# Warm-up matmuls that read a preamble constant and last until x arrives, and a 384 + 256 split of the last output projection

## The chip, the cores and the metric

The kernel runs on one core of a Trainium2 chip. The metric is the device time of one execution in microseconds (us), the slowest core's, which here is the only one. Several executions of each kernel were timed; all of them count as fast runs (each lists a mean granted clock of 1.0).

## The reference

A gate mixes two branches of the same input x (2048 tokens of 640 features, bf16). Branch A is a diagonal complex state-space recurrence (P = 640 states) with an output projection; branch B is a two-layer network with a hidden width of 1728.

```python
g = sigmoid((x * gate_w).sum(-1, keepdims=True))
# A: Lam_bar = exp(dt * Lam); h_t = Lam_bar * h_{t-1} + B_bar x_t
#    y = 2 * Re(C h) + x * Dskip
# B: b = gelu(x @ w1 + b1) @ w2 + b2
return g * a + (1 - g) * b          # bf16, [1, 2048, 640]
```

## The kernel before

Every operation is recorded with its reads and writes. A small list scheduler orders the operations of each engine before anything is emitted, and semaphore waits follow from the reads and writes. Four parts matter here.

The first loads. `xtrans` is a transposing DMA of some 128-feature slices of x; `w1load(k, ...)` loads slice k of w1, its first 1024 columns, 256 KB. SP is SyncE, which issues DMAs.

```python
w1load(0, "act", -101)               # ScalarE's queue
xtrans(0, [0], 0, 1.27)              # all else on SP's queue, in this order
xtrans(0, [1, 2], 1, 1.27)
w1load(1, "sp", 2)
w1load(2, "sp", 3)
xtrans(0, [3, 4], 4, 1.27)
w1load(3, "sp", 5)
w1load(4, "sp", 6)
# ... five small loads into `rows` (Lambda, log_dt, b1) on ScalarE's queue
```

The warm-up: eight matmuls on zeros, which VectorE writes first. Their result is never read.

```python
wz = SB("wz", [128, 512], BF16)
def f_wz():
    return inc("dve", nc.vector.memset(wz[:, :], 0.0))
op("wz", "dve", 0.35, (), ["wz"], f_wz, prio=-70)

def f_warm():
    t = None
    for _ in range(8):
        t = nc.tensor.matmul(PS[6][:, :], wz[:, 0:128], wz[:, :], start=True, stop=True)
    return inc("pe", t)
op("warm", "pe", 3.2, ["wz"], [("bank", 6)], f_warm, prio=-1000)
```

The first real matmuls go slice by slice through x (k outer, eight output banks inner), so that TensorE can start with slice 0. Seven of them need only slice 0. After these comes `cols`, one small matmul that transposes `rows`; then those that need slice 1.

```python
seq = [(k, jf) for k in range(KD) for jf in range(NW)]
seq.remove((0, NW - 1))
seq.insert(seq.index((1, NW - 1)), (0, NW - 1))
# ... one matmul PS[jf] += W1sb[k, jf].T @ xT[0][k] for each
op("cols", "pe", 0.3, list(ROWS) + ["b1b", "ident"], [("bank", 7)], f_cols, prio=7.5)
```

The end. For the last chunk of 128 tokens, each half of the output projection (ten accumulating matmuls) is evicted by VectorE, which adds what was prepared before (`E2`), and is stored at once.

```python
# HALF = 320; NCH - 1 is the last chunk
for hf in range(2):
    cols = slice(hf * HALF, (hf + 1) * HALF)
    def f_fin(hf=hf, cols=cols):
        return inc("dve", nc.vector.scalar_tensor_tensor(
            out=osb[c % NO][:, cols], in0=PS[cbank[hf]][:, 0:HALF], scalar=gcol[:, c:c + 1],
            in1=E2[c % NE][:, cols], op0=ALU.mult, op1=ALU.add))
    def f_st(hf=hf, cols=cols):
        return dma_inc("sp", nc.sync.dma_start(o2[c * 128:(c + 1) * 128, cols], osb[c % NO][:, cols]), f"stl{hf}")
```

## Time and profile before

| | us |
|---|---|
| median of 3 executions | 214.95 (214.95 to 215.01) |
| span of the profiled execution | 213.84 |
| start of TensorE's dense run | 7.39 |
| start of the last VectorE operation | 211.61 |
| from there to the end of the span | 2.23 |

The page's busy times (busy us, share of the span, instructions), and, further down on it, its chain that ended last by engine. PE is TensorE's matmuls, PEld its weight loads, DVE VectorE, ACT ScalarE.

```profile
PE 210.0 (98%) x1257; PEld 119.3 (56%) x1257; DVE 188.3 (88%) x260; ACT 112.9 (53%) x205; POOL 2.5 (1%) x10
...
PE 95%; DMA 2%; SPq 1%; DVE 0%; issue 0%
```

TensorE bounds the kernel; only the first 7.4 us and the last 2.2 are anything else. The beginning of the chain in order of time (start in us, duration in us, what):

```profile
2.03 1.29 SPq L332
3.32 0.05 issue
3.37 3.89 DMA W1sb<-in_B_w_dram
7.26 0.14 issue
7.39 7.28 PE ps L598 x33
```

SP issues the transposing loads first, so the load of W1 slice 1 is issued at 3.37 and lands at 7.26; TensorE's unbroken work starts 0.13 us later. What TensorE did until then, from the timeline (start, duration, engine, line, operation, tiles, count, idle time before and what ended it):

```profile
1.19 0.13 PEld L400 LDWEIGHTS ps<-wz 128*128 128x128 bf16 x2 [1.19 <-DVE wz L393]
...
1.20 3.59 PE L400 MATMUL ps<-wz 128*128 128x512 bf16 x8 [1.20 <-DVE wz L393]
...
4.81 0.13 PEld L598 LDWEIGHTS ps<-xT,W1sb 128*128 128x128 bf16 x2 [0.93 <-DMA xT<-in_A_x_dram]
...
5.22 0.15 PEld L598 LDWEIGHTS ps<-xT,W1sb 128*128 128x128 bf16 x1 [0.27 <-issue]
5.65 0.81 PEld L598 LDWEIGHTS ps<-xT,W1sb 128*128 128x128 bf16 x4 [0.28 <-issue]
...
6.79 0.22 PE L410 MATMUL ps<-ident,rows 128*128 128x128 bf16 x1
...
7.39 6.85 PE L598 MATMUL ps<-xT,W1sb 128*128 128x512 bf16 x31 [0.39 <-DMA W1sb<-in_B_w_dram]
```

The weight loads show the clock. While they come one each 0.43 us and take 0.15 us, TensorE runs slow; four of them within 0.81 us, as from 5.65 on, are fast (all but the first of these take 0.10 us). The trace's own clock record has the full clock from 5.76. All eight matmuls that can go ahead are through by 7.0; then TensorE waits for W1 slice 1. And the end of the timeline:

```profile
208.69 2.88 PE L791 MATMUL ps<-CT,H 128*128 128x320 bf16 x20
...
210.25 0.55 DVE L824 SCALAR_TENSOR_TENSOR osb<-ps,gcol,E 128x320 bf16<-128x320 f32 x1 [0.31 <-PE ps L791]
210.83 1.69 SPq L830 DMA_DIRECT2D out_dram<-osb  x2
211.61 0.55 DVE L824 SCALAR_TENSOR_TENSOR osb<-ps,gcol,E 128x320 bf16<-128x320 f32 x1 [0.81 <-PE ps L791]
```

(A line with x2 or more is merged: the SP line spans both store issues.)

### The profile page before, as it was taken

What the parts mean: (1) busy time and instruction counts of PE and PEld (TensorE: products, weight loads), DVE (VectorE), ACT (ScalarE), POOL (GpSimd) and SP (SyncE); (2) the same over time, 40 slices, a digit from 0 to 9 for tenths busy, and PEclk for the clock granted to TensorE, in tenths of its full rate; (3) what the DMA queues carried; (4) which work ended last, traced back from release to release, by engine and by line L of the source; (5) the groups of instructions that cost most, each with busy time, mean ns of one, the idle gap of its engine ahead of it and who ended that gap; (6) DMA issues with size and microseconds to landing.
All of it is one profiled execution on the core that took longest, in us unless ns stands there. A gap on an engine that the chain in (4) does not pass through costs nothing.

```text
span 213.8 us, 3098 instructions
## 1 busy us (share of the span) xinstructions
PE 210.0 (98%) x1257; PEld 119.3 (56%) x1257; DVE 188.3 (88%) x260; ACT 112.9 (53%) x205; POOL 2.5 (1%) x10
## 2 busy tenths in 40 slices
PE   7999999999999999999999999999999999999995
PEld 2344444444567675444467767444446777677673
DVE  1599999999999899999999999499999999988612
ACT  2569556679525334557835332556786554535230
POOL 1000000000000100000000010000000000000000
PEclk9999999999999999999999999999999999999999
DMA  7999699999000140000000023000000010000011
GB/s 138 297 271 192 142 364 271 224 191 204 0 0 3 61 153 3 31 0 0 0 3 31 0 49 138 32 0 0 3 0 2 0 34 31 31 34 31 31 34 31
DMA packets 30874, 16.35 MB, mean 76 GB/s; under 512 B 23948, under 2 KB 29964, under 8 KB 30860
## 3 DMA queue, kind: packets, MB, share of 16 engines
q1 hardware_dynamic: 30368, 14.57, 28.7%
q0 software_dynamic: 288, 1.31, 2.0%
q10 hardware_dynamic: 204, 0.27, 0.5%
q8 instruction: 10, 0.16, 0.4%
q14 instruction: 4, 0.03, 0.0%
HBM read 7.63 MB, written 2.62 MB: 48 GB/s over the span
## 4 chain that ended last, share of the span: by engine, by line
PE 95%; DMA 2%; SPq 1%; DVE 0%; issue 0%
PE ps L745 26%; PE ps L618 22%; PE ps L791 21%; PE ps L658 20%; PE ps L598 3%; DMA W1sb<-in_B_w_dram 2%; PE ps L759 1%; SPq L332 1%; PE ps L636 1%; DVE osb L824 0%
## 5 line engine op out<-in xcount | busy, mean ns | idle before, releaser
L745 PE MATMUL ps<-W2sb,Gl 128*128 128x320 bf16 x416 | 59.1, 299 | 0.0
L745 PEld LDWEIGHTS ps<-W2sb,Gl 128*128 128x128 bf16 x416 | 40.6, 98 | 16.5 <-ACT Gl L625 0.4
L618 PE MATMUL ps<-xT,W1sb 128*128 128x512 bf16 x220 | 48.1, 379 | 0.0
L791 PE MATMUL ps<-CT,H 128*128 128x320 bf16 x320 | 46.1, 299 | 0.0
L698 DVE TENSOR_TENSOR_SCAN W<-atab,V 128x1280 bf16<-128x1280 f32 x16 | 44.3, 2811 | 0.3
L658 PE MATMUL ps<-xT,BT 128*128 128x512 bf16 x200 | 43.8, 379 | 0.0
L773 ACT ACTIVATE E<-ps,g1col 128x320 bf16<-128x320 f32 x32 | 16.1, 526 | 42.2 <-PE ps L759 18.3
L791 PEld LDWEIGHTS ps<-CT,H 128*128 128x128 bf16 x320 | 30.7, 98 | 13.5 <-issue 1.8
L618 PEld LDWEIGHTS ps<-xT,W1sb 128*128 128x128 bf16 x220 | 21.5, 98 | 25.9
L625 ACT ACTIVATE Gl<-ps,cols 128x512 bf16<-128x512 f32 x44 | 29.7, 691 | 11.5 <-PE ps L618 11.5
L658 PEld LDWEIGHTS ps<-xT,BT 128*128 128x128 bf16 x200 | 19.4, 98 | 23.5 <-ACT Gl L625 0.4
L667 ACT ACTIVATE U<-ps 128x512 bf16<-128x512 f32 x40 | 23.6, 595 | 15.7 <-PE ps L658 15.6
L802 ACT ACTIVATE E<-ps,gcol 128x320 bf16<-128x320 f32 x30 | 15.7, 528 | 16.7 <-PE ps L791 16.6
L732 ACT ACTIVATE ps<-b2b 128x320 f32<-128x320 bf16 x32 | 14.0, 440 | 0.9
L460 DVE TENSOR_TENSOR osb<-xg,E 128x640 bf16<-128x640 bf16 x15 | 7.3, 487 | 7.8 <-ACT E L802 6.8
L810 DVE SCALAR_TENSOR_TENSOR xg<-xn,gcol,dsk 128x640 bf16<-128x640 bf16 x16 | 13.8, 882 | 0.4
L575 DVE SCALAR_TENSOR_TENSOR scr<-xn,gwb 128x640 bf16<-128x640 bf16 x16 | 13.2, 823 | 0.4
L460 DVE TENSOR_TENSOR H<-H,V 128x1280 bf16<-128x1280 bf16 x16 | 12.5, 821 | 0.3
L460 DVE TENSOR_TENSOR V<-V,W 128x1280 bf16<-128x1280 bf16 x16 | 12.5, 821 | 0.3
L460 DVE TENSOR_TENSOR V<-mr,U 128x2560 bf16<-128x2560 bf16 x8 | 11.9, 1489 | 0.2
L460 DVE TENSOR_TENSOR H<-c,W 128x2560 bf16<-128x2560 bf16 x8 | 11.9, 1488 | 0.1
L460 DVE TENSOR_TENSOR V<-s,W 128x2560 bf16<-128x2560 bf16 x8 | 11.9, 1484 | 0.0
(77 smaller groups left out, 101.2 us busy)
## 6 DMA issues: line engine op xcount, KB each, us to landing
out_dram<-osb SPq DMA_DIRECT2D x15, 160.0 KB, 1.8
W2sb<-in_B_w_dram SPq DMA_DIRECT2D x1, 2080.0 KB, 12.2
xn<-in_A_x_dram SPq DMA_DIRECT2D x2, 640.0 KB, 6.4
xn<-in_A_x_dram POOLq DMA_DIRECT2D x2, 640.0 KB, 4.8
W1sb<-in_B_w_dram SPq DMA_DIRECT2D x4, 256.0 KB, 4.1
W1sb<-in_B_w_dram SPq DMA_DIRECT2D x1, 880.0 KB, 6.1
W1sb<-in_B_w_dram ACTq DMA_DIRECT2D x1, 256.0 KB, 2.8
gwb<-in_gate_w_dram SPq DMA_DIRECT2D x1, 160.0 KB, 5.2
```

What stands on the lines that cost most here:

```text
L460: return inc("dve", nc.vector.tensor_tensor(out=o, in0=a, in1=b, op=o_))
L618: t = nc.tensor.matmul(PS[bank][:, :], W1sb[:, k, jf * 128:(jf + 1) * 128], xT[q][:, k, :], start=(k == 0), stop=(k == KD - 1))
L625: return inc("act", nc.scalar.activation(Gl[q % 2][:, jf, :], PS[bank][:, :], ACT.Gelu_apprx_tanh, bias=b1col[:, jf:jf + 1]))
L658: t = nc.tensor.matmul(PS[bank][:, :], BT[:, ci, kd, k * 128:(k + 1) * 128], xT[q][:, kd, :], start=(kd == 0), stop=(kd == KD - 1))
L667: return inc("act", nc.scalar.activation(dst, src, ACT.Copy, scale=1.0 if ci == 0 else -1.0))
L698: t = inc("dve", nc.vector.tensor_tensor_scan(out=g[:, ci, :], data0=a, data1=v[:, ci, :], initial=0.0, op0=ALU.mult, op1=ALU.add))
L732: return inc("act", nc.scalar.activation(PS[bank][:, 0:HALF], b2b[:, cols], ACT.Copy))
L745: t = nc.tensor.matmul(PS[bank][:, 0:HALF], Gl[q % 2][:, jf, t4 * 128:(t4 + 1) * 128], W2sb[:, jf, cols], start=False, stop=False, skip_gr ...
L773: return inc("act", nc.scalar.activation(E1[c % NE][:, cols], PS[bank][:, 0:HALF], ACT.Copy, scale=g1col[:, c:c + 1]))
L791: t = nc.tensor.matmul(PS[bank][:, 0:HALF], H[b % NHB][:, ci, k, s * 128:(s + 1) * 128], CT[:, ci, k, cols], start=(i == 0), stop=(i == 2 ...
L802: return inc("act", nc.scalar.activation(E2[c % NE][:, cols], PS[bank][:, 0:HALF], ACT.Copy, scale=gcol[:, c:c + 1]))
L810: return inc("dve", nc.vector.scalar_tensor_tensor(out=xg[c % 2][:, :], in0=xn[q % 2][:, c % 4, :], scalar=gcol[:, c:c + 1], in1=dsk[:, :] ...
```

## The change

The intent has two parts. The warm-up is to start as soon as TensorE may, without VectorE's memset, by reading a constant 1.0 that the preamble writes anyway, and it is to last until x is there, so that the clock does not meet a gap. At the end, the last part that is evicted and stored is to be smaller (256 instead of 320 columns), since its eviction and its store are followed by nothing that could hide them.

```diff
-        wz = SB("wz", [128, 512], BF16)
-        def f_wz():
-            return inc("dve", nc.vector.memset(wz[:, :], 0.0))
-        op("wz", "dve", 0.35, (), ["wz"], f_wz, prio=-70)
+        one = nc.const_aps.tensor(1.0, [128, 1], BF16)
 
         def f_warm():
             t = None
-            for _ in range(8):
-                t = nc.tensor.matmul(PS[6][:, :], wz[:, 0:128], wz[:, :], start=True, stop=True)
+            for n in (512,) * 9 + (192,):
+                t = nc.tensor.matmul(PS[6][:, 0:n], one.broadcast_to([128, 128]), one.broadcast_to([128, n]), start=True, stop=True)
             return inc("pe", t)
-        op("warm", "pe", 3.2, ["wz"], [("bank", 6)], f_warm, prio=-1000)
+        op("warm", "pe", 3.9, (), [("bank", 6)], f_warm, prio=-1000)
# ... cproj: the last chunk alone
+        CCOLS = (slice(0, D - 256), slice(D - 256, D))
-                cols = slice(hf * HALF, (hf + 1) * HALF)
+                cols = CCOLS[hf] if c == NCH - 1 else slice(hf * HALF, (hf + 1) * HALF)
+                n = cols.stop - cols.start
# ... 0:HALF becomes 0:n in its matmuls; f_fin and f_st use CCOLS[hf];
# ... fin{hf} names both halves of E2 as read
```

More of the change, by code (lines that the diff above doesn't have):

```diff
@@ L783, in cproj, with f_mm @@
                 cbank[hf] = bank
-                cols = slice(hf * HALF, (hf + 1) * HALF)
-                def f_mm(bank=bank, cols=cols):
+                cols = CCOLS[hf] if c == NCH - 1 else slice(hf * HALF, (hf + 1) * HALF)
+                n = cols.stop - cols.start
+                def f_mm(bank=bank, cols=cols, n=n):
                     t = None
@@ L790, in f_mm @@
                         for k in range(KP):
-                            t = nc.tensor.matmul(PS[bank][:, 0:HALF], H[b % NHB][:, ci, k, s * 128:(s + 1) * 128], CT[:, ci, k, cols],
+                            t = nc.tensor.matmul(PS[bank][:, 0:n], H[b % NHB][:, ci, k, s * 128:(s + 1) * 128], CT[:, ci, k, cols],
                                                  start=(i == 0), stop=(i == 2 * KP - 1))
@@ L794, in f_mm @@
                     return inc("pe", t)
-                op(f"c_{c}_{hf}", "pe", 2 * KP * d_mm(HALF), [("H", b % NHB), ("CT", 0), ("CT", 1)], [("bank", bank)], f_mm, prio=pe_prio())
+                op(f"c_{c}_{hf}", "pe", 2 * KP * d_mm(n), [("H", b % NHB), ("CT", 0), ("CT", 1)], [("bank", bank)], f_mm, prio=pe_prio())
                 if c == NCH - 1:
@@ L820, in comb @@
                 for hf in range(2):
-                    cols = slice(hf * HALF, (hf + 1) * HALF)
+                    cols = CCOLS[hf]
                     def f_fin(hf=hf, cols=cols):
-                        return inc("dve", nc.vector.scalar_tensor_tensor(out=osb[c % NO][:, cols], in0=PS[cbank[hf]][:, 0:HALF], scalar=gcol[:, c:c + 1],
+                        return inc("dve", nc.vector.scalar_tensor_tensor(out=osb[c % NO][:, cols], in0=PS[cbank[hf]][:, 0:cols.stop - cols.start], scalar=gcol[:, c:c + 1],
                                                                         in1=E2[c % NE][:, cols], op0=ALU.mult, op1=ALU.add))
-                    op(f"fin{hf}", "dve", d_dve(HALF), [("bank", cbank[hf]), ("E2", c % NE, hf)], [("osb", c % NO, hf)], f_fin, prio=-60)
+                    op(f"fin{hf}", "dve", d_dve(HALF), [("bank", cbank[hf]), ("E2", c % NE, 0), ("E2", c % NE, 1)], [("osb", c % NO, hf)], f_fin, prio=-60)
                     def f_st(hf=hf, cols=cols):
```

## The prediction

> **What bounds the kernel now.** TensorE. The page gives PE 98% busy of a 213.8 us span; the chain that ended last is 95% PE, which runs from 7.39 us to about 211.6 without a wait. The change touches only the two ends.
>
> *Front.* In the chain of waits the first 7.4 us are not PE: two transposing loads are issued on SP (0.75 to 3.32 us), a W1sb load is issued at 3.37 and landed by 7.26, PE starts at 7.39. The timeline shows the warm-up inside that time: 8 matmuls from 1.20 us (released by the memset of wz on VectorE), one each 0.43 us; x is there at 4.81. The weight loads tell the clock: 0.15 us each until 5.65, then 0.10, and from there matmuls come 0.21 us apart. So two or three of the seven real matmuls that need only the first slices of x and W1 run slow. Still all seven are through by about 6.8, the small transposing matmul by 7.0, and PE then waits 0.39 us for the second W1 slice. The Trainium skill ("TensorE: Matmul & The Clock Gate", Part 1) says that the clock is released after about 3.4 us of sustained activity, in a free-running window; this trace has 4.4 us from the first warm-up matmul to the fast rate.
>
> *Tail.* The last 20 matmuls start at 208.7, 0.136 us each for 320 columns, and end at 211.6; VectorE's last operation takes 0.551 us (211.61 to 212.16); the store is issued at 212.19 and lands 1.6 us later, which ends the span.
>
> **What the change does.**
> 1. The wz memset (0.27 us) and the wait for it go. PE may start at about 0.85 to 0.95, some 0.3 us earlier. 9.4 matmuls at 0.427 are 4.0 us, so warm-up ends at about 4.9, just past 4.81. Real matmuls may begin up to 0.1 us later, or the fast clock may come 0 to 0.3 us earlier. Neither is on the chain: the second W1 slice decides at 7.26, with about 0.4 us to spare. Worth: 0.0 us. If the window's phase differs between executions, those where the fast clock came too late would lose less; three runs within 0.06 us show no such spread.
> 2. Last chunk at 384 + 256 columns: the same columns in total, so PE still ends at about 211.6 (256 columns need 0.109 us, above the 0.098 us of a weight load). The first eviction becomes about 0.62 us, 210.5 to 211.1, off the chain. The last shrinks by 64 columns: 640 columns of this operation on bf16 take 0.882, 320 take 0.551, so an estimated 1.03 ns a column, or 0.066 us: 0.551 to about 0.485. The last store is 64 KB instead of 80 KB; its data move in about 0.4 us of the 1.6, so up to 0.05 us less.
>
> Sum: 0.07 to 0.12 us off 214.95.
>
> **Predicted: 214.85 us, range 214.5 to 215.1.** Chances: faster by over 2% 0.005, within 2% 0.99, slower by over 2% 0.005.
>
> **What would show it.** Warm-up from about 0.9 to 4.9, no gap before the first real matmul; fast matmuls from 5.3 to 5.7; PE still waiting for the second W1 slice and starting its unbroken run at 7.4 (within 0.05). Last VectorE operation 0.48 to 0.49 us; last landing 1.55 to 1.6 us; span 213.7.
>
> **What would make it wrong.** The dense run starts clearly before 7.3: a load was held up by something that the change moved. Or the fast clock comes after about 6.5, by another phase of its window: real matmuls run slow past 7.3 and some tenths of a us are lost, in either kernel. Or the 256-column matmuls do not hide their weight loads and the second half takes over 1.1 us. Or the last store is not shorter, or the two stores collide.

## The result, and the profile after

Four executions of each kernel: 215.14 us median after (214.96 to 215.35), 214.98 before (214.95 to 215.29). The ratio is 1.0005 with a 95% interval of 0.9987 to 1.0022: the same. Ratios here are the mean time of one kernel's fast runs over that of the other's in the same rounds, so they are not quite the ratio of the medians quoted. The four executions after had spans of 214.0, 214.0, 213.6 and 213.6 us; the profiled one is one of the longer.

The page after, busy times:

```profile
PE 210.2 (98%) x1249; PEld 119.7 (56%) x1259; DVE 188.0 (88%) x259; ACT 112.9 (53%) x205; POOL 2.5 (1%) x10
```

The beginning of the chain after:

```profile
2.03 1.28 SPq L332
3.32 0.05 issue
3.37 4.23 DMA W1sb<-in_B_w_dram
7.60 0.14 issue
7.73 6.85 PE ps L593 x31
```

The chain is the same chain. W1 slice 1, again issued at 3.37, landed at 7.60 instead of 7.26, and the dense run started 0.34 us later. The front of the timeline:

```profile
0.75 0.14 PEld L395 LDWEIGHTS ps<-const-bfloat16-1.0 128*128 128x128 bf16 x2 [0.75 <-issue]
...
0.78 4.16 PE L395 MATMUL ps<-const-bfloat16-1.0 128*128 128x512 bf16 x10 [0.78 <-PEq L930]
...
4.71 0.17 PEld L593 LDWEIGHTS ps<-xT,W1sb 128*128 128x128 bf16 x2 [0.41 <-DMA xT<-in_A_x_dram]
...
6.01 0.15 PEld L593 LDWEIGHTS ps<-xT,W1sb 128*128 128x128 bf16 x1 [0.28 <-issue]
6.44 0.39 PEld L593 LDWEIGHTS ps<-xT,W1sb 128*128 128x128 bf16 x2 [0.28 <-issue]
...
7.17 0.22 PE L405 MATMUL ps<-ident,rows 128*128 128x128 bf16 x1
...
7.73 6.63 PE L593 MATMUL ps<-xT,W1sb 128*128 128x512 bf16 x30 [0.35 <-DMA W1sb<-in_B_w_dram]
```

The warm-up does what it was meant to: it starts at 0.78 instead of 1.20 and goes on to 4.94, past the arrival of x. Yet the fast clock came later in this execution, after the weight load at 6.44 (the clock record says 6.59), not before 5.9. Even so TensorE was through with its eight early matmuls by about 7.4 and still waited for the load. The end:

```profile
209.03 2.88 PE L788 MATMUL ps<-CT,H 128*128 128x384 bf16 x20
...
210.86 0.62 DVE L821 SCALAR_TENSOR_TENSOR osb<-ps,gcol,E 128x384 bf16<-128x384 f32 x1 [0.57 <-PE ps L788]
211.50 1.29 SPq L827 DMA_DIRECT2D out_dram<-osb  x2
211.95 0.48 DVE L821 SCALAR_TENSOR_TENSOR osb<-ps,gcol,E 128x256 bf16<-128x256 f32 x1 [0.47 <-PE ps L788]
```

From the start of the last VectorE operation to the end of the span it is now 214.04 - 211.95 = 2.09 us, 0.14 less than before. Between the dense run's start and that operation both kernels take the same time to the hundredth: 211.61 - 7.39 = 211.95 - 7.73 = 204.22. So the span is a sum of three terms, and only two of them differ:

| | dense run starts | middle | end | span |
|---|---|---|---|---|
| before | 7.39 | 204.22 | 2.23 | 213.84 |
| after | 7.73 | 204.22 | 2.09 | 214.04 |

### The profile page after: what moved, and what is told of

The parts are those of the page before. It is cut to its first block, busy times and chain, and to the rows that moved or that the text cites. A ratio compares the mean times of both kernels' runs of the same rounds, so it can differ in the third digit from the quotient of the medians.

```text
span 214.0 us, 3091 instructions
## 1 busy us (share of the span) xinstructions
PE 210.2 (98%) x1249; PEld 119.7 (56%) x1259; DVE 188.0 (88%) x259; ACT 112.9 (53%) x205; POOL 2.5 (1%) x10
## 4 chain that ended last, share of the span: by engine, by line
PE 95%; DMA 2%; SPq 1%; issue 0%; DVE 0%
PE ps L740 26%; PE ps L613 22%; PE ps L788 21%; PE ps L653 20%; PE ps L593 3%; DMA W1sb<-in_B_w_dram 2%; PE ps L754 1%; SPq L332 1%; PE ps L631 1%; DVE osb L821 0%
## 5 line engine op out<-in xcount | busy, mean ns | idle before, releaser
L613 PE MATMUL ps<-xT,W1sb 128*128 128x512 bf16 x215 | 47.5, 379 | 0.3
L788 PE MATMUL ps<-CT,H 128*128 128x320 bf16 (+2 forms) x320 | 46.2, 299 | 0.0
L653 PE MATMUL ps<-xT,BT 128*128 128x512 bf16 x196 | 43.1, 379 | 0.3 <-issue 0.2
L613 PEld LDWEIGHTS ps<-xT,W1sb 128*128 128x128 bf16 x220 | 21.5, 98 | 26.0
L455 DVE TENSOR_TENSOR W<-mi,U 128x2560 bf16<-128x2560 bf16 x8 | 11.9, 1484 | 0.0
```

Of the source, the lines that this page charges most:

```text
L455: return inc("dve", nc.vector.tensor_tensor(out=o, in0=a, in1=b, op=o_))
L613: t = nc.tensor.matmul(PS[bank][:, :], W1sb[:, k, jf * 128:(jf + 1) * 128], xT[q][:, k, :], start=(k == 0), stop=(k == KD - 1))
L653: t = nc.tensor.matmul(PS[bank][:, :], BT[:, ci, kd, k * 128:(k + 1) * 128], xT[q][:, kd, :], start=(kd == 0), stop=(kd == KD - 1))
L788: t = nc.tensor.matmul(PS[bank][:, 0:n], H[b % NHB][:, ci, k, s * 128:(s + 1) * 128], CT[:, ci, k, cols], start=(i == 0), stop=(i == 2 * K ...
```

## The experiments

Theory A: the shorter end is real and is there in every execution, but the start differs between executions by more than that, for reasons that the change does not touch: above all the landing of W1 slice 1, and perhaps the moment of the fast clock. Theory B: the new warm-up itself delays the start (through the loads or the clock) and so eats the gain. A third, theory C, came up with the second set: the spread comes from elsewhere and the landing only goes along with it. The twelve runs were made in three sets of four; the four kernels of a set ran on one chip and share the executions of the kernel before.

### 1. The split alone (t_only)

```diff
 # the changed kernel, with wz, its memset and the eight matmuls of before put back
```

> Split of the last projection alone, warm-up of before. Theory A (the tail is really shorter by 0.13 us in every execution, and what hides it is a start that differs between executions for reasons that the change does not touch: when the second W1 slice lands and when the fast clock comes): from the start of the last VectorE operation to the end of the span 2.09 us as in the changed kernel (before: 2.23), dense run starting anywhere from 7.2 to 7.8 us, ratio to before 0.9985 to 1.0005. Theory B (the new warm-up itself delays the start by some 0.3 us and eats the gain): dense run at 7.4 as before, every execution 0.13 us faster than before, ratio 0.9994 or less.

Measured: ratio 0.9992 (0.9974 to 1.001); 215.11 us median (214.67 to 215.82), before 215.22 (214.73 to 215.73, 11 executions). The profiled execution was the slowest of its six. The beginning of its chain:

```profile
3.36 4.61 DMA W1sb<-in_B_w_dram
7.97 0.14 issue
8.11 7.28 PE ps L598 x33
```

This is the old warm-up, and the latest landing: 7.97. The fast clock was early this time (seven weight loads within 1.20 us from 4.76 on), so TensorE stood idle for 1.6 us waiting for the load. The end was 2.09 us. A slow start therefore needs no new warm-up.

### 2. The warm-up alone (w_only)

```diff
 # the kernel before, with the new warm-up in place of wz; 320 + 320 columns kept
```

> New warm-up alone, 320 + 320 columns at the end. Theory A: tail 2.23 us as before; the dense run starts 0.10 to 0.14 us after the later of two things, the landing of the second W1 slice and the end of the first seven matmuls and the small transposing one; ratio 0.999 to 1.001. Theory B: executions gather 0.3 us above before's usual time, about 215.3, ratio 1.001 to 1.002, and the dense run starts at 7.7 again.

Measured: ratio 0.9995 (0.998 to 1.001), 215.2 us median (214.84 to 215.4). Load landed at 7.29, dense run at 7.43, end 2.23 us. The beginning of its chain:

```profile
3.37 3.92 DMA W1sb<-in_B_w_dram
7.29 0.14 issue
7.43 7.28 PE ps L593 x33
```

The new warm-up did not bring 7.7 back, and theory B's 1.001 to 1.002 was not met. Theory A's reading holds: the run starts 0.14 us after the landing.

### 3. The changed kernel again (after_again)

```diff
 # none: the changed kernel, unaltered
```

> The changed kernel once more, beside the others. Theory A: executions spread from about 214.9 to 215.4 as the first time, the profiled one starts its dense run at another time than 7.73, and the fast clock comes at another time than 6.59 us[...]. Theory B: 7.7 again, clock at 6.6 again.

Measured: ratio 0.9995 (0.9977 to 1.0013), 215.09 us median (214.72 to 215.86). The same program now had its load at 7.38, its dense run at 7.51 and its fast clock at about 4.8 (the first two real matmuls start 0.26 us apart, all later ones 0.22), against 7.60, 7.73 and 6.59 the first time. Landing and clock vary between executions of one program, and not together: the clock came about 1.8 us earlier, the load 0.22.

### 4. No warm-up at all (no_warm)

```diff
-        def f_warm(): ...
-        op("warm", "pe", 3.9, (), [("bank", 6)], f_warm, prio=-1000)
```

> The changed kernel without any warm-up matmul. PE then starts with x at 4.7 us, slow[...]. Up to the fast clock each matmul takes 0.427 instead of 0.214 us. Seven plus the transposing one are then through at about 7.9, so the start of the dense run moves to 7.9 to 8.0 and matmuls from there to the fast clock lose half their time: 0.4 + 0.1 to 1.8 us slower than the changed kernel, ratio to before 1.002 to 1.010. If it is not slower, the warm-up has no worth at all here and the clock does not matter.

Measured: ratio 1.003 (1.0014 to 1.0047), 215.93 us median (215.37 to 216.37). The weight loads of its timeline:

```profile
4.77 0.13 PEld L583 LDWEIGHTS ps<-xT,W1sb 128*128 128x128 bf16 x2 [4.77 <-DMA xT<-in_A_x_dram]
...
7.32 0.15 PEld L395 LDWEIGHTS ps<-ident,rows 128*128 128x128 bf16 x1 [0.28 <-issue]
...
8.28 0.15 PEld L583 LDWEIGHTS ps<-xT,W1sb 128*128 128x128 bf16 x1 [0.28 <-issue]
8.70 3.21 PEld L583 LDWEIGHTS ps<-xT,W1sb 128*128 128x128 bf16 x15 [0.27 <-issue]
```

Here the load landed at 7.54, but TensorE came out of its slow matmuls only at 7.85, and a few more ran slow after that (the middle term is 204.72 instead of 204.22). So a warm-up is worth about 0.8 us in this kernel: 215.93 us median against 215.09 with the new warm-up in the same set. The old one already had all of that: t_only, with the old warm-up and the new end, had 215.11.

### 5. W1 slice 1 issued early, old warm-up and old end (w1_early_old)

```diff
-        w1load(1, "sp", 2)
+        w1load(1, "act", -100.5)
```

> The kernel before with one load moved: the second W1 slice is issued on ScalarE's queue right behind the first, at about 1.2 us instead of 3.4. Theory A (its landing sets the start of the dense run, and its spread is most of the spread between executions): it lands before 6.5 us, the dense run starts when PE is through with the first eight matmuls, between 6.2 and 7.4[...]; 0.3 to 0.9 us faster than before, ratio 0.996 to 0.9985; a later load does not take the gain back. Theory C (the spread comes from elsewhere, the landing only goes along with it): no gain, ratio 0.9995 to 1.0005. The risk: the load shares the DMA engines with the first slice of x and delays it.

### 6. The same load moved in the changed kernel (w1_early_new)

The edit is that of 5, in the changed kernel. What theory A expects to come 0.42 us earlier ("it") is the fast clock.

> The same moved load in the changed kernel, so that the warm-up is no longer hidden behind the load. Theory A: [...]starting 0.42 us earlier brings it 0.42 earlier on average, worth half of that (0.2 us) once it is exposed, and the tail 0.13: 0.15 to 0.45 us faster than the same with the old warm-up and the old tail, ratio to before 0.994 to 0.998. Theory B (new warm-up delays the start): no faster than w1_early_old.

Measured: ratios 1.0008 (0.9995 to 1.002) for the old and 1.0003 (0.999 to 1.0015) for the new; 215.54 and 215.29 us median. Both expectations failed. The load did land earlier, at 4.96 and 5.20, but x came later (TensorE's first real weight load at 5.44 and 5.50 instead of 4.8; x slices 1 and 2 at 6.28 and 6.38 instead of 5.80 in the kernel before), as did the small loads into `rows`. Of the waits of w1_early_new between 4 and 9 us (engine, line and what it waited for, us in total, times, longest):

```profile
PE ps L593 <- DMA xT<-in_A_x_dram: 1.0, 1, 1.0
...
PE ps L405 <- DMA rows<-in_B_b_dram: 0.3, 1, 0.3
```

L405 is the small transposing matmul. It stands in front of the slice-1 matmuls in TensorE's order, waited for its own loads (the last landed at 7.24), and the dense run began behind it, at 7.66. The wait was not removed; it was handed to the next load. As TensorE waited again in w1_early_new, this pair does not test the warm-up.

### 7. W1 slice 1 issued between the transposing loads (w1_sp_new)

```diff
-        xtrans(0, [1, 2], 1, 1.27)
-        w1load(1, "sp", 2)
+        w1load(1, "sp", 1)
+        xtrans(0, [1, 2], 2, 1.27)
```

> In the changed kernel the second W1 slice is issued on SP between the two first transposing loads of x, at about 2.0 us. It lands about 1 us earlier than before, 6.3 to 6.8, and the next x slices some 0.5 us later, at about 6.3. Theory A: dense run at 6.5 to 7.3, between the changed kernel and w1_early_new; ratio to before 0.996 to 0.999.

Measured: ratio 0.999 (0.9977 to 1.0002), 215.04 us median (214.71 to 215.28). In the profiled execution the load landed at 5.56, earlier than the 6.3 to 6.8 expected, and the dense run began at 6.97: the start can be moved by this load, though by less than the load itself. From its chain:

```profile
2.98 3.58 DMA rows<-in_B_b_dram
7.03 6.80 PE ps L593 x31
...
14.28 5.57 PE ps L613 x25
```

What came last before the dense run were other loads: the last small one into `rows` (6.56; the transposing matmul waited 1.0 us for it) and x slices 1 and 2 (6.76). And the middle grew by 0.19 us (204.41): the last matmul of slice 4 starts at 13.88, and the next one, 0.40 us later at 14.28 instead of 0.22, needs the remainder of W1, which landed at 14.23 (13.01 in the kernel before). The executions still spread over 0.57 us, though W1 slice 1 no longer decided the start in the profile. So the landing of this one load is not the whole of the spread; the rest was not taken apart further.

### 8. 448 + 192 columns (split448)

```diff
-        CCOLS = (slice(0, D - 256), slice(D - 256, D))
+        CCOLS = (slice(0, D - 192), slice(D - 192, D))
```

> The changed kernel with 448 + 192 columns in the last chunk. The last VectorE operation shrinks by another 64 columns to 0.42 us. A 192-column matmul needs 0.080 us, below the 0.098 of a weight load, so the last ten matmuls take 0.98 instead of 0.80 if weight loads bound them: the PE part of the end grows by 0.18, the rest shrinks by 0.07 and up to 0.03 at the store. From the start of the last ten matmuls to the end of the span: 0.98 + 2.0. Net 0.05 to 0.1 us slower than 384 + 256. If weight loads hide all the same, 0.07 to 0.13 faster.

Measured: ratio 1.0004 (0.999 to 1.0018), 215.31 us median (214.82 to 215.72); start at 7.29, middle 204.22, end 2.00 us. The end of the timeline:

```profile
208.58 2.88 PE L788 MATMUL ps<-CT,H 128*128 128x448 bf16 x20
...
210.68 1.24 DVE L821 SCALAR_TENSOR_TENSOR osb<-ps,gcol,E 128x448 bf16<-128x448 f32 x2 [0.84 <-PE ps L788]
211.39 0.89 SPq L827 DMA_DIRECT2D out_dram<-osb  x2
```

My main expectation was wrong: the weight loads do not bound the 192-column matmuls. In the trace the last ten start 0.082 to 0.083 us apart although each weight load still takes 0.098 us, so successive loads overlap. The other case came true: 0.09 us shorter than 384 + 256. With 320, 256 and 192 columns last, the end is a series:

| last part | last VectorE operation | from its end to the end of the span | end in all |
|---|---|---|---|
| 320 columns | 0.55 | 1.68 | 2.23 |
| 256 columns | 0.48 | 1.61 | 2.09 |
| 192 columns | 0.42 | 1.58 | 2.00 |

The executions' times do not resolve 0.14 or 0.23 us. All 31 executions of the kernel before in these three sets have a mean of 215.20 and a standard deviation of 0.27 us, so the mean of six is good to about 0.27 / sqrt(6) = 0.11 us. That the end is shorter is shown by the traces, where it repeats to 0.02 us; the times are only compatible with it.

### 9 to 11. TensorE freed from both waits, with three warm-ups (exp_old, exp_new, exp_none)

The load is moved as in 5, and the transposing matmul is put behind the fourth matmul of slice 1 after the scheduler has ordered everything, so that nothing else changes its place. exp_old has the old warm-up and the old end, exp_new the new ones, exp_none no warm-up and the new end.

```diff
         order = pr.sch.order()
+        pe = order["pe"]
+        cols_op = next(i for i in pe if i.name == "cols")
+        pe.remove(cols_op)
+        pe.insert(next(n for n, i in enumerate(pe) if i.name == "m1_0_4_1"), cols_op)
```

> Like w1_early_old, and the small transposing matmul put behind four matmuls of the second slice, because there it waited for its five small loads and held up the dense run. Old warm-up, old tail. PE should then run from the arrival of x (about 5.4) without a stop, so that each slow matmul counts. [...]the loss is 0 to 1.3 us; ratio to before 0.998 to 1.001, spread of the executions 1 us or more.

> The same with the new warm-up and the new tail. Theory A: 0.13 us from the tail and 0.1 to 0.2 on average from a clock that comes 0.42 us earlier: 0.1 to 0.4 us faster than exp_old, ratio 0.9965 to 0.9995. Theory B (the new warm-up delays): no faster than exp_old.

> The same with no warm-up at all, the new tail. [...]1.2 to 2.9 us slower than exp_new, ratio to before 1.005 to 1.013. That would say what warm-up is worth once nothing hides it; hidden (run no_warm) it was 0.8.

Measured, in one set, against 215.05 us before:

| | median us | all | ratio | interval |
|---|---|---|---|---|
| exp_old | 215.09 | 214.95 to 215.56 | 1.0000 | 0.9985 to 1.0014 |
| exp_new | 215.20 | 214.77 to 217.0 | 1.0010 | 0.9981 to 1.0038 |
| exp_none | 216.75 | 216.12 to 217.37 | 1.0072 | 1.0053 to 1.0091 |

In all three profiles TensorE ran without a stop once x was there, at 5.39, 5.57 and 5.36. Nothing was won, since x came 0.6 us later than in the kernel before. With the waits gone, the absence of a warm-up costs 216.75 - 215.20 = 1.55 us, twice what it cost when hidden (1.17 us by the means, because of one slow execution of exp_new). Between the two warm-ups the set decides nothing: exp_new was expected 0.1 to 0.4 us faster than exp_old and its median was 0.11 slower; one of its six executions took 217.0 and its interval covers both. In the profiled pair the new one was fast from the first real weight load on, the old one only after 6.64, but run 3 shows that this differs between executions of one kernel. Whether the earlier warm-up helps on average once it is exposed stays open.

### 12. The helpful parts together (best)

The edits of 7, 8 and 9 in the changed kernel.

> The changed kernel with the three things that helped: the second W1 slice issued between the transposing loads, the transposing matmul behind four matmuls of that slice, and 448 + 192 columns. Tail from the start of the last VectorE operation 2.00 us (0.23 less than before); matmuls of the second slice from 6.6 to 7.1. Ratio to before 0.9955 to 0.9985. If the start gives nothing it is the tail alone, 0.9989.

Measured: ratio 0.999 (0.9972 to 1.0007), 214.9 us median (214.63 to 215.7) against 215.05. The end was 2.00 us as expected; the expected gain at the start did not come. The profiled execution was the slowest of the six, and its waits of TensorE between 4 and 25 us show where such a start ends up:

```profile
PE ps L613 <- DMA W1sb<-in_B_w_dram: 0.4, 1, 0.4
PE ps L593 <- DMA xT<-in_A_x_dram: 0.3, 1, 0.3
PE ps L593 <- DMA W1sb<-in_B_w_dram: 0.2, 1, 0.2
```

The matmuls of slice 1 began at 7.13, after a wait for x slices 1 and 2, which landed at 7.08 (W1 slice 1 had been there since 5.96). Then the last of the five W1 slices was waited for (landed at 12.94, matmuls at 12.99), then the remainder of W1 (L613; landed at 15.23 instead of 13.0 in the kernel before). Of slice 4, fifteen of 16 completions were there by 10.88; the last one alone came 2.06 us later. Earlier matmuls reach the later loads sooner, and in this profile these loads came later too. It is not shown to beat either kernel.

## Why the prediction was right or wrong

**The size of the whole: right in kind.** I predicted 0.1 us less than 214.95 in a program that would stay within 2%, and the kernels are the same within 0.2% either way. My range ended at 215.1; the median of the four executions was 215.14, the ratio times the earlier median is 1.0005 x 214.95 = 215.06. Which side of 215.1 a median of four falls on is luck: single executions of the kernel before have a standard deviation of 0.27 us, more than the gain that I forecast. Only the terms of the sum can be judged.

**The warm-up is worth 0.0 us: right.** In six of the seven profiles of kernels with unmoved loads the dense run starts 0.13 to 0.14 us after W1 slice 1 lands, with either warm-up; the seventh has no warm-up.

| profile | warm-up | W1 slice 1 landed | dense run | fast clock | end |
|---|---|---|---|---|---|
| before | old | 7.26 | 7.39 | 5.7 to 5.9 | 2.23 |
| after | new | 7.60 | 7.73 | 6.4 to 6.7 | 2.09 |
| t_only | old | 7.97 | 8.11 | about 4.8 | 2.09 |
| w_only | new | 7.29 | 7.43 | 5.6 to 5.9 | 2.23 |
| after_again | new | 7.38 | 7.51 | about 4.8 | 2.09 |
| split448 | new | 7.15 | 7.29 | 4.7 to 5.1 | 2.00 |
| no_warm | none | 7.54 | 7.85 | 8.7 to 8.9 | 2.09 |

The starting time was right in its mechanism, and my figure a little late: 0.78 where I had 0.85 to 0.95; the warm-up ended at 4.94 where I had 4.9.

**The step that failed: "three runs within 0.06 us show no such spread".** Three executions that agree are no proof that the front is steady. The kernel before itself spread from 214.73 to 215.73 over 31 executions. I had allowed for one cause of spread, the clock, and had taken the other, the landing of W1 slice 1 at 7.26, for a constant ("the second W1 slice decides at 7.26", "unbroken run at 7.4 (within 0.05)"). It landed between 7.15 and 7.97 in the seven profiles above. The trace has the load's 16 completions: the last but one came at 6.90 to 7.23 in all seven, and only the last one strays, by 0.03 us (before) to 0.77 us (t_only) behind it. Why that one is late was not found. The whole 0.34 us by which the profile after starts later than the profile before is this term, and it covers the gain at the other end.

**The fast clock "from 5.3 to 5.7": wrong, by the risk that was named.** It came 5.8 us after the first warm-up matmul in the profile after (6.59 less 0.78) and about 4.0 us after it in the same program's second profile. The Trainium skill says in "TensorE: Matmul & The Clock Gate", Part 1, that the window is free-running and does not reset when a kernel starts, and that the ramp should not be fitted to a specific count. These traces agree that the time varies: about 3.6 us (t_only) to 5.8 us in the kernels of the table that have a warm-up. In w1_sp_new it was shorter still: the warm-up matmul that starts at 3.61, 2.83 us after the first one at 0.78, is already fast. So the 3.4 us of sustained activity that the prediction took from this page is no lower bound here. I had quoted the page and then given a range of 0.4 us. It cost nothing, since even the late clock left TensorE waiting for the load.

**The end: right in mechanism, a little small.** I gave 0.07 to 0.12 us, and the profile shows 0.14. The eviction term was exact (0.066 predicted, 0.551 to 0.484 measured). The mis-sized term is the store: "up to 0.05 us less", measured 1.68 to 1.61, 0.07 us. The 256-column matmuls did hide their weight loads, and the two stores did not collide.

**Theory B falls** in the profiles: the warm-up alone starts at 7.43, and the old warm-up has the latest start of all. Single profiles could mislead here, since the start strays; the spans of all executions of the first set say the same. With the middle taken as 204.22 us and the end as in the table, an estimate of the mean start is 7.41 us for the twelve executions with the new warm-up and 7.48 for the seventeen with the old one, a difference of 0.06 us with a standard error of 0.12; theory B asked for 0.3 us the other way. Theory C is partly right: run 7 moved the landing by 1.7 us, to where it no longer decided the start of the profiled execution, and the spread stayed, so other terms of the start spread as well.

## What to carry to other kernels

Write the span as start + dense middle + end, and read each term in several profiles before believing a difference of a tenth of a microsecond: here the start differed by up to 0.8 us between profiles of kernels with a warm-up and unmoved loads, and the end repeated to 0.02. A warm-up matters as a whole (0.8 us hidden, 1.5 exposed), but refining it is worth nothing while the first unhidden load lands later than TensorE is ready; and behind that load stood others (runs 5 to 7 and 12), so moving it alone won little. At the end of a kernel, the columns of the last eviction and store are paid in full, so make the last part small, as long as the earlier part's eviction is through by then.

## What the Trainium skill lacked or had wrong

- "TensorE: Matmul & The Clock Gate", Part 2, "Back-to-back issue gap": it gives about 131 ns a matmul as the sustained rate at 512 columns in a stream of weight loads and matmuls and says that its isolated formula N/2.4 + 2.5 over-counts there. Here 65 such matmuls, each with its own weight load, took 14.03 us in the chain of before, 216 ns each, which is the formula's value (215.8). At 320 columns 26 took 3.53 us, 136 ns each (formula 135.8), and at 192 columns they start 82 to 83 ns apart (formula 82.5).
- The same page, "LDWEIGHTS": it gives P / 1.2, 107 ns for 128 columns; the trace shows 98 ns at the fast clock. With 192 columns the matmuls followed each other faster than one weight load takes (82.5 ns against 98, split448).
- "DMA: Bandwidth & Descriptors", "Why a DMA increments its semaphore by 16 and not by 1": it says that the 16 engines finish independently, but not how far apart. In seven profiles of one 256 KB load the last of the 16 completions trailed the last but one by 0.03 to 0.77 us, and in six of them it decided when TensorE could start; in best the last completion of W1 slice 4 trailed by 2.06 us.
- The same page, "Anatomy of one DMA": it fits a fixed cost of about 2.0 us for DMAs issued from GpSimd, and gives no such sum for those issued from SP. The last stores here, of 80, 64 and 48 KB, landed 1.6, 1.5 and 1.5 us after their issue.
